# A fourth unit of the sequence DFT as block products, and four weight units prepared in the feed-forward

## The chip, the core and the metric

The kernel runs on one core of one Trainium2 chip. The time is the device time of one execution in microseconds, as the median of several runs; lower is better. The engines are TensorE (PE in the profile, its weight loads PEld), VectorE (DVE), ScalarE (ACT), GpSimd (POOL) and SyncE (SP), which here only issues DMAs, all from one queue in order.

## What is computed

One layer: an FNet mixing step and a gated feed-forward, each behind a layer norm and with a residual. There are 2048 tokens of 448 features, 1792 hidden features, all float32.

```python
def _A_ref(x, dft_seq_re, dft_seq_im, dft_hid_re, dft_hid_im):
    a = jnp.einsum("bsd,ed->bse", x, dft_hid_re)
    b = jnp.einsum("bsd,ed->bse", x, dft_hid_im)
    return jnp.einsum("ts,bse->bte", dft_seq_re, a) - jnp.einsum("ts,bse->bte", dft_seq_im, b)

def _B_ref(x, w_gate, w_up, w_down):
    g = jnp.einsum("bsd,df->bsf", x, w_gate)
    u = jnp.einsum("bsd,df->bsf", x, w_up)
    return jnp.einsum("bsf,fd->bsd", _gelu(g) * u, w_down)

h = x + _A_ref(_layernorm(x, axis=-1), ...)
h2 = h + _B_ref(_layernorm(h, axis=-1), ...)
```

## The kernel before

**Numbers.** Every float32 operand of a matmul is split into a high and a low float16 part: ACT writes the high part (`hi_part`, L100), DVE the low part as the source less the high part (`lo_part`, L104 without and L106 with a scale). A product is three matmuls: high by high, high by low, low by high.

**First step.** The tokens are 16 tiles of 128, taken in pairs; a pair is a unit u of 0 to 7, in the order 0, 1, 5, 2, 6, 3, 7, 4 (`ORDER`). A tile is normed, split, transposed, and multiplied by the hidden DFT (`feature_mm`, L421, result `ab`), and `feature_out` writes its float16 operands `b`.

**Sequence DFT.** It has eight passes p of 256 output tokens; each pass adds up, over the eight units u, a block of DFT weights `w_seq` (raw `wr`, split `ws`) times that unit's `b` (`seq_mm`, L517). A unit has one of two forms:

- plain: 24 matmuls of 448 columns; its weights are four blocks and are split as they are (1024 columns on ACT and on DVE);
- in `S_UNITS` (units 5, 6, 7): seven block products in the manner of Strassen, 42 matmuls of 224 columns. DVE first adds up four of seven weight blocks (`seq_sums`, three instructions, L479 to L481, tile `wsum`); the split covers seven blocks (256, 512 and 1024 columns). In the first step such a unit's tiles go to a float32 tile `b32` in the pool `ring` (tag `w`, two buffers), POOL makes four sums of blocks (`feature_sums`, L459 to L461), and the split covers seven blocks (1568 columns) where a plain tile's covers 2 x 448.

**Order.** All of this is a list of slots: `("F", i)` for tile i of the first step and `("U", p, u)` for a unit of a pass. Units of pass 0 stand between the F slots. `plan(n, rank, what)` puts work ahead of slot n; a unit's sums are planned three slots ahead, its split two slots ahead, its load six. The order so written is the order on every engine.

**Gate and up weights.** They come in 14 units f of 128 hidden features. For each, `Weights(f)` fetches raw weights (two DMAs, tile `gu_raw`), `sums` makes block sums on DVE (tile `gu_s`, L579 to L582), `split` writes both halves (tile `gu_w`, in `ring`, the one that `b32` uses too), and `store` writes the result to `w_dram`. All 14 are planned into the first step and the DFT: one early (unit 13, four slots behind the second seven-product unit), the others spread evenly from three slots behind the first step's end.

**Feed-forward.** It has four quarters q of 512 tokens and 14 units f in each, so tiles t = 0 to 55; tile t has three accumulators X, Y, Z (L927). `gw[t]` holds its weights: the first three are left from the DFT, the others are loaded from `w_dram` (`gw_load`). In the first quarter eight of them pass through a buffer `ahead` of four places, which has the size of a quarter's hidden values `hh`. The down product (L869) starts with the second quarter; in the first, `down_prep` prepares its weights: POOL makes sums (`wd_s`, L210 to L213), ACT and DVE split. In the first quarter the body of tile t is:

```python
cur.x_close()      # X += ...; ACT: gelu of X (g1)
nxt.x_open()       # X of t+1; ACT: copy it into Y of t+1 (L966)
prev.c_last()
cur.y_mid()        # Y += ...; ACT: u3; DVE: hidden values
nxt.z_open()
nxt.y_open()       # Y of t+1 += ...
cur.y_close()
cur.z_close()
down_prep(t - 1)   # at odd t: ACT splits wd and, once POOL is done, wd_s
```

(comments added here). X, Y and Z alternate between two sets of banks from tile to tile.

Of the kernel before, what the change touches and what calls it, by code (L numbers as in the profile page):

```python
# [8 lines left out]
F16 = mybir.dt.float16  # L9
F32 = mybir.dt.float32  # L10
# [3 lines left out]
P = 128  # L14
S, D, DF = 2048, 448, 1792
NT = S // P
NF = DF // P
# [10 lines left out]
W_SC = 256.0  # L28
# [4 lines left out]
def kernel(  # L33
# [37 lines left out]
    nc = tc.nc  # L71
# [9 lines left out]
    ps_dft = right.enter_context(tc.tile_pool(name="ps_dft", bufs=4, space=bass.MemoryType.PSUM))  # L81

    ident = const.tile([P, P], F16, name="ident")
# [15 lines left out]
    def hi_part(dst, src, scale=1.0):  # L99
        A.activation(dst, src, AF.Copy, scale=scale)  # L100
# [67 lines left out]
    def w_tile(name, pool):  # L168
        return pool.tile([P, 28 * P], F16, tag="w", bufs=2 if pool is ring else 1, name=name)
# [119 lines left out]
    dft = right.enter_context(tc.tile_pool(name="dft", bufs=1, side="right"))  # L289

    N_PASS, N_UNIT = 8, 8
    S_UNITS, WR = (5, 6, 7), 3
# [5 lines left out]
    first = ExitStack()  # L298
    p2 = right.enter_context(tc.tile_pool(name="p2", bufs=1, side="right"))
    p1 = first.enter_context(tc.tile_pool(name="p1", bufs=1, side="right"))  # L300
# [262 lines left out]
    def h_store(p):  # L563
        nc.sync.dma_start(h_dram[p], hp[divmod(p, 2)])


    class Weights:


        def __init__(self, f):  # L570
            self.f = f
            self.raw = p2.tile([P, 2, 6, P], F32, tag="raw", name=f"gu_raw{f}")
            for r in range(2):
                nc.sync.dma_start(self.raw[:, r], w_gu[f, :, r])

        def sums(self):
            gate, up = self.raw[:, 0], self.raw[:, 1]
            s = self.s = p2.tile([P, 10, P], F32, tag="s", name=f"gu_s{self.f}")
            V.tensor_add(s[:, 0:3], up[:, 0:3], up[:, 3:6])  # L579
            V.tensor_sub(s[:, 3:6], s[:, 0:3], gate[:, 0:3])  # L580
            V.tensor_sub(s[:, 6:8], gate[:, 0:2], up[:, 0:2])
            V.tensor_sub(s[:, 8:10], gate[:, 4:6], s[:, 4:6])  # L582
# [14 lines left out]

        def split(self, of_raw):
            if of_raw:
                self.w = w_tile(f"gu_w{self.f}", ring if self.f != 2 else ring3)  # L600
# [23 lines left out]
    for n, s in zip((2, 5, 7), S_UNITS):  # L624
        mixed.insert(n, s)
# [4 lines left out]
    gu = {}  # L630
# [5 lines left out]
    def plan(n, rank, *what):  # L636
        at(todo, n, *((rank, w) for w in what))
# [43 lines left out]
    plan(0, 9, lambda: gu.update({order[0]: Weights(order[0])}))  # L681
    for k, f in enumerate(order):
        n = at_f[k]
        plan(n, 7, lambda f=f: gu[f].sums())
        plan(n + 1, 7, lambda f=f: gu[f].split(True))
        if k + 1 < NF:
            plan(n + 2, 9, lambda f=order[k + 1]: gu.update({f: Weights(f)}))
        plan(n + 2, 7, lambda f=f: gu[f].split(False))
        plan(n + 3, 10, lambda f=f: gu[f].store())
# [112 lines left out]
    for n in sorted(todo):  # L802
        for _, what in sorted(todo.pop(n), key=lambda t: t[0]):
            what()
    seq_out(N_PASS - 1)
    h_store(N_PASS - 1)
    down_load(1)
    gw = {f: gu[f].w for f in range(3)}
    right.close()


    right.close()
# [65 lines left out]
    fpool = ctx.enter_context(tc.tile_pool(name="fpool", bufs=1, side="right", reuse_waits="tile"))  # L878
# [129 lines left out]
    ahead = fpool.tile([P, 4, 28 * P], F16, tag="hh", bufs=2, name="gw_ahead")  # L1008

    def gw_load(t):  # L1010
        if 3 <= t < 7 or 10 <= t < 14:
            gw[t] = ahead[:, (t - 3) % 7]
        else:
            gw[t] = w_tile(f"gw{t}", ring if t % 3 else ring3)
        nc.sync.dma_start(gw[t], w_dram[t % NF])

# [52 lines left out]
    def last_begin():  # L1069
        last["h"] = fpool.tile([P, 2, NF, 2 * TQ], F16, tag="hh", bufs=2, name="h_last")  # L1070
# [118 lines left out]
    for t in range(3, 7):  # L1189
        gw_load(t)  # L1190
# [7 lines left out]
    for t in range(N_GU):  # L1198
        q, f = divmod(t, NF)
        if f == 0 and q < 3:  # L1200
            hh[q] = fpool.tile([P, NC, 4, TQ], F32, tag="hh", bufs=2, name=f"hh{q}")
            if 1 <= q <= 2:
                hops_tile(q + 1)
        if 0 < t < 8:
            gw_load(t + 6)
        if NF - 2 <= t < N_GU - 2:
            gw_load(t + 2)
# [12 lines left out]
        if q == 0:  # L1220
# [4 lines left out]
            cur.y_mid()  # L1225
            nxt.z_open()
# [4 lines left out]
            if t > 0:  # L1231
                down_prep(t - 1)
        else:
# [100 lines left out]
```

## Time and profile before

| | |
|---|---|
| runs | 718.6, 719.0, 719.13 us; median 719.0 |
| profiled execution | 718.65 us, span 716.9 us |
| PE busy | 709.5 us, 5800 matmuls |
| PEld, DVE, ACT, POOL busy | 562.2, 500.0, 386.1, 203.2 us |
| DMA | 142.89 MB, mean 199 GB/s |
| granted clock of PE | 1.00 throughout |

The span goes from the first to the last instruction; the profiled execution's own time holds some 1.75 us more around it. A timeline row reads: start, length, engine, line, operation, output tile and inputs, shape, count, and in brackets the idle time of that engine just before, with what ended it. A row with a count covers several instructions.

### The profile page before, as it was taken

Reading aid. Unit: us, or ns where it says so; the run is one execution under the profiler, and the core shown is the slowest. Engines: PE = TensorE matmul, PEld = TensorE weight load, DVE = VectorE, ACT = ScalarE, POOL = GpSimd, SP = SyncE. Lnnn points to the kernel's source line nnn. Section 1 sums busy time; section 2 is a strip of 40 time slices with the busy share of each in tenths; the row PEclk is TensorE's granted clock in tenths of the full one; section 3 lists DMA queues with packets and bytes.
Section 4 is the critical chain, followed back from the end, with each engine's and each line's share of the span. In section 5 each row is a group of like instructions: output and inputs, shape, how many; then the busy total and the mean of one; then the engine's idle time right before and its main releaser. Section 6 shows DMA issues by size and latency. Waiting matters only on the chain.

```text
span 716.9 us, 14587 instructions
## 1 busy us (share of the span) xinstructions
PE 709.5 (99%) x5800; PEld 562.2 (78%) x5800; DVE 500.0 (70%) x1016; ACT 386.1 (54%) x818; POOL 203.2 (28%) x235
## 2 busy tenths in 40 slices
PE   8999999999999999999999999999999999999998
PEld 5556556676767666676788889999999999999998
DVE  6777859898989887888345667575765756677520
ACT  5575644765665654646155565555555545555500
POOL 0023120000000000010015564374664755557230
PEclk9999999999999999999999999999999999999999
DMA  9464444896969699685089525647466576655401
GB/s 329 105 147 94 106 152 143 298 264 250 306 232 307 232 272 351 215 305 172 1 336 354 187 101 161 190 163 203 174 188 194 187 215 209 212 179 206 155 15 65
DMA packets 72339, 142.89 MB, mean 199 GB/s; under 512 B 41296, under 2 KB 47568, under 8 KB 72272
## 3 DMA queue, kind: packets, MB, share of 16 engines
q1 hardware_dynamic: 72272, 141.97, 61.3%
q8 instruction: 45, 0.74, 0.4%
q14 instruction: 22, 0.18, 0.1%
HBM read 112.46 MB, written 20.19 MB: 185 GB/s over the span
## 4 chain that ended last, share of the span: by engine, by line
PE 83%; DVE 8%; ACT 5%; DMA 2%; issue 1%; SPq 0%; ACTq 0%; DVEq 0%
PE acc L517 36%; PE pY L927 14%; PE acc_d L869 11%; PE pZ L927 9%; PE pX L927 9%; ACT b L100 1%; DVE xs L104 1%; PE last_Z L1098 1%; PE last_X L1098 1%; PE last_Y L1098 1%; DVE st_x L327 1%; ACT x L354 1%; ACT xs L100 1%; DMA w_dram<-gu_w 1%; DMA wh_raw<-in_w_hid_dram 1%
## 5 line engine op out<-in xcount | busy, mean ns | idle before, releaser
L517 PE MATMUL acc<-b,ws 128*128 128x448 f16 (+1 forms) x1968 | 279.4, 305 | 0.2 <-DVE ws L106 0.2
L517 PEld LDWEIGHTS <-ws 128*128 128x128 f16 x1968 | 190.4, 98 | 88.7 <-DVE ws L106 0.8
L927 PEld LDWEIGHTS <-gw 128*128 128x128 f16 x1755 | 171.5, 98 | 17.7 <-issue 0.8
L927 PE MATMUL pY<-hops,gw 128*128 128x256 f16 x765 | 105.2, 273 | 0.0
L869 PE MATMUL acc_d<-wd,dn_w 128*128 128x224 f16 x882 | 105.1, 259 | 0.0
L100 ACT ACTIVATE ws<-wr 128x1024 f16<-128x1024 f32 (+2 forms) x88 | 64.3, 756 | 46.9 <-issue 26.2
L869 PEld LDWEIGHTS <-dn_w 128*128 128x128 f16 x882 | 85.1, 98 | 2.8
L106 DVE SCALAR_TENSOR_TENSOR ws<-wr,ws 128x1024 f16<-128x1024 f32 (+2 forms) x88 | 73.8, 861 | 19.1 <-ACT ws L100 18.5
L1006 POOL TENSOR_TENSOR hh<-hh,c 128x256 f32<-128x256 f32 x42 | 31.8, 759 | 141.9 <-ACT c L1004 141.9
L210 POOL TENSOR_TENSOR wd_s<-wd 128x448 f32<-128x448 f32 x7 | 7.9, 1134 | 224.8 <-DMA w_dram<-gu_w 207.8
L927 PE MATMUL pZ<-hops,gw 128*128 128x256 f16 x495 | 68.7, 273 | 0.4 <-DVE hh L937 0.3
L927 PE MATMUL pX<-hops,gw 128*128 128x256 f16 x495 | 68.4, 273 | 0.0
L421 PEld LDWEIGHTS <-xT 128*128 128x128 f16 x352 | 34.2, 98 | 32.7 <-issue 1.5
L104 DVE TENSOR_TENSOR dn_w<-hh,dn_w 128x256 f16<-128x256 f32 x42 | 19.6, 466 | 53.1 <-ACT dn_w L100 53.1
L1029 POOL TENSOR_TENSOR dn_s<-hh 128x256 f32<-128x256 f32 x42 | 52.9, 1258 | 0.0
L971 ACT ACTIVATE u<-pY 128x256 f32<-128x256 f32 x56 | 21.5, 384 | 55.7 <-PE pY L927 55.6
L104 DVE TENSOR_TENSOR dn_w<-dn_s,dn_w 128x640 f16<-128x640 f32 x42 | 46.3, 1102 | 6.2 <-ACT dn_w L100 5.0
L966 ACT ACTIVATE pY<-pX 128x256 f32<-128x256 f32 x56 | 20.7, 369 | 49.2 <-PE pX L927 49.1
L421 PE MATMUL ab<-wh_hi,xT 128*128 128x448 f16 x224 | 45.6, 352 | 0.6 <-ACT xT L384 0.4
L1028 POOL TENSOR_TENSOR dn_s<-hh 128x256 f32<-128x256 f32 x42 | 38.0, 904 | 0.0
L985 ACT ACTIVATE u<-pY 128x256 f32<-128x256 f32 x56 | 21.5, 383 | 26.9 <-PE pY L927 26.6
L860 POOL TENSOR_TENSOR hr<-hr,v 128x224 f32<-128x224 f32 x48 | 33.4, 717 | 0.1
(137 smaller groups left out, 971.2 us busy)
## 6 DMA issues: line engine op xcount, KB each, us to landing
gw<-w_dram SPq DMA_DIRECT2D x45, 896.0 KB, 5.0
wr<-in_w_seq_dram SPq DMA_DIRECT2D x64, 512.0 KB, 4.6
w_dram<-gu_w SPq DMA_DIRECT2D x14, 896.0 KB, 7.5
gu_raw<-in_w_gu_dram SPq DMA_DIRECT2D x28, 384.0 KB, 5.6
gw_ahead<-w_dram SPq DMA_DIRECT2D x8, 896.0 KB, 7.5
wd<-in_w_down_dram SPq DMA_DIRECT2D x14, 448.0 KB, 4.4
hx<-in_x_dram SPq DMA_DIRECT2D x8, 448.0 KB, 6.9
h_dram<-hx SPq DMA_DIRECT2D x8, 448.0 KB, 6.8
```

What stands on the lines that cost most here:

```text
L100: A.activation(dst, src, AF.Copy, scale=scale)
L104: V.tensor_sub(dst, src, hi)
L106: V.scalar_tensor_tensor(dst, src, scale, hi, op0=ALU.mult, op1=ALU.subtract)
L421: PE.matmul(feat[i][r][:, :D], xT[i][:, kx, :], w[:, kw, r * D : (r + 1) * D], start=n == 0, stop=n == 10,)
L517: PE.matmul(banks[k][:, cols], lhs, rhs, start=k not in begun, stop=stop, skip_group_check=True)
L860: op(x, x, m)
L869: PE.matmul(acc[k // 2][:, k % 2 * HD : (k % 2 + 1) * HD], a_of(la, a), b_of(lb, b), start=first and m == 0 and k % 2 == 0, stop=last and ...
L927: PE.matmul(ps, w[:, wl, wa + ws, :], ops[:, m + ms, :], start=first and n == 0, stop=last and n == len(terms) - 1, skip_group_check=True,)
L1006: G.tensor_mul(c22, c22, self.c12)
L1028: G.tensor_add(s[:, 0:2], t[:, 0:2], t[:, 2:4])
L1029: G.tensor_sub(s[:, 2:4], t[:, 1:4:2], t[:, 0:4:2])
L1098: PE.matmul(banks[0][:, c * HD : (c + 1) * HD] if one else banks[c][:, 0:HD], last["h"][:, lh, f, tok], w, start=f == 0 and m == 0 and c = ...
```

## The change

`S_UNITS` becomes (4, 5, 6, 7), so unit 4, the last of the first step, takes the seven-product form. In a pass the units now stand as 0, 1, 4, 2, 5, 3, 6, 7 (before: 0, 1, 5, 2, 3, 6, 4, 7). Its larger operands need room. So the gate/up units 4, 7, 10 and 13 are no longer prepared in the DFT: they are prepared in the first quarter, from tiles t = 0, 3, 6 and 9 on, in six beats each, two per tile (`late_prep`, `Weights.beat`), and are used where they were made as well as stored. The buffer `ahead` goes away; a pool `scr` holds raw weights, sums and two weight tiles in the first quarter, and the second quarter's hidden values take its place (`odd_q`). In the DFT two gate/up units (12 and 11) are early, and the other eight are spread from 15 slots behind the first step's end. The transposing constant `ident` moves to a pool that is closed after the first step.

```diff
-    S_UNITS, WR = (5, 6, 7), 3
+    S_UNITS, WR = (4, 5, 6, 7), 3
...
+        def beat(self, k):
+
+            if k < 2:
+                self.sums(k == 0, k == 1)
+            if k == 1:
+                self.w = self.w_of()
+            parts = self.parts(True) + self.parts(False)
+            if k > 1:
+                s0, s1, src = parts[k - 2]
+                lo_part(self.slots(1, s0, s1, src), src, self.slots(0, s0, s1, src), W_SC)
+            if 0 < k < 5:
+                s0, s1, src = parts[k - 1]
+                hi_part(self.slots(0, s0, s1, src), src, W_SC)
...
-    for n, s in zip((2, 5, 7), S_UNITS):
+    for n, s in zip((2, 4, 6, 7), S_UNITS):
...
-    early_f = [s + 4 for s in pairs[1:2]]
-    n0 = p1_end + 3
-    order = list(reversed(range(2, NF))) + [0, 1]
-    late_f = NF - len(early_f)
+    early_f = [s + 4 for s in pairs[1:3]]
+    n0 = p1_end + 15
+    LATE = {4: 0, 7: 6, 10: 12, 13: 18}
+    in_dft = [f for f in range(NF) if f not in LATE]
+    N_DFT = len(in_dft)
+    order = list(reversed(in_dft[2:])) + in_dft[:2]
...
+    fpool = ctx.enter_context(tc.tile_pool(name="fpool", bufs=1, side="right", reuse_waits="tile"))
+    quarter0 = ExitStack()
+    scr = quarter0.enter_context(tc.tile_pool(name="scr", bufs=1, side="right", reuse_waits="tile"))
+
+    def gw_tile(t):
+        name = f"gw{t}"
+        if t < NF and t % 5 >= 3:
+            return w_tile(name, scr) if t % 5 == 3 else scr.tile([P, 28 * P], F16, tag="stage", name=name)
+        return w_tile(name, ring3 if (t % 5 == 2 if t < NF else t % 3 == 1) else ring)
...
+    gw_load(3)
     seq_out(N_PASS - 1)
+    gu_late(min(LATE))
     h_store(N_PASS - 1)
     down_load(1)
...
-    for t in range(3, 7):
-        gw_load(t)
+    late_beats = {n + k: (f, k) for f, n in LATE.items() for k in range(6)}
...
+        f, k = late_beats[beat]
+        gu[f].beat(k)
+        after = [v for v in LATE if v > f]
+        if k == 3 and after:
+            gu_late(after[0])
+        if k == 5:
+            gu[f].store()
+            gw[f] = gu[f].w
...
-            hh[q] = fpool.tile([P, NC, 4, TQ], F32, tag="hh", bufs=2, name=f"hh{q}")
+            if q == 1:
+                quarter0.close()
+                odd_q = ctx.enter_context(tc.tile_pool(name="odd_q", bufs=1, side="right"))
+            hh[q] = (fpool, odd_q)[q % 2].tile([P, NC, 4, TQ], F32, tag="hh", name=f"hh{q}")
...
-        if 0 < t < 8:
-            gw_load(t + 6)
-        if NF - 2 <= t < N_GU - 2:
-            gw_load(t + 2)
+        ahead = {1: 5, 2: 6, 4: 8, 5: 9, 7: 11, 8: 12, 10: 14, 12: 15, 13: 16}.get(t) if t <= NF else t + 2
+        if ahead and ahead < N_GU:
+            gw_load(ahead)
...
             cur.y_mid()
+            late_prep(2 * t)
             nxt.z_open()
             nxt.y_open()
             cur.y_close()
@@
             if t > 0:
                 down_prep(t - 1)
+            late_prep(2 * t + 1)
```

DVE's order at the end of the first step, before, from pass 1's unit 0 on. In the names, `ws0_7` is the split weight of pass 0, unit 7, `b8` and `b9` are the operands of unit 4's tiles 8 and 9, and the numbers behind are running ones.

```order
L106 SCALAR_TENSOR_TENSOR ws1_0_1183<-wr1_0_770,ws1_0_1183 128x1024
L479 TENSOR_TENSOR wsum0_7_1186<-wr0_7_912 128x512
L480 TENSOR_TENSOR wsum0_7_1186<-wsum0_7_1186,wr0_7_912 128x256
L481 TENSOR_TENSOR wsum0_7_1186<-wsum0_7_1186,wr0_7_912 128x256
L106 SCALAR_TENSOR_TENSOR b9_1216<-ab9_0_1192,b9_1216 128x448
L106 SCALAR_TENSOR_TENSOR b9_1216<-ab9_1_1193,b9_1216 128x448
L106 SCALAR_TENSOR_TENSOR ws0_7_1221<-wr0_7_912,ws0_7_1221 128x256
L106 SCALAR_TENSOR_TENSOR ws0_7_1221<-wr0_7_912,ws0_7_1221 128x512
L106 SCALAR_TENSOR_TENSOR ws0_7_1221<-wsum0_7_1186,ws0_7_1221 128x1024
L106 SCALAR_TENSOR_TENSOR ws0_4_1258<-wr0_4_1033,ws0_4_1258 128x1024
```

The same place in the changed kernel, from the last piece of unit 7's split on (ahead of that split the four sums of gate/up unit 11, L581 to L587, now stand):

```order
L111 SCALAR_TENSOR_TENSOR ws0_7_1225<-wsum0_7_1187,ws0_7_1225 128x1024
L109 TENSOR_TENSOR b8_1232<-b32_8_1178,b8_1232 128x1568
L480 TENSOR_TENSOR wsum0_4_1238<-wr0_4_1033 128x512
L481 TENSOR_TENSOR wsum0_4_1238<-wsum0_4_1238,wr0_4_1033 128x256
L482 TENSOR_TENSOR wsum0_4_1238<-wsum0_4_1238,wr0_4_1033 128x256
L111 SCALAR_TENSOR_TENSOR gu_w11_1242<-gu_raw11_1035,gu_w11_1242 128x512
L111 SCALAR_TENSOR_TENSOR gu_w11_1242<-gu_raw11_1035,gu_w11_1242 128x256
L111 SCALAR_TENSOR_TENSOR ws0_4_1277<-wr0_4_1033,ws0_4_1277 128x256
L111 SCALAR_TENSOR_TENSOR ws0_4_1277<-wr0_4_1033,ws0_4_1277 128x512
L111 SCALAR_TENSOR_TENSOR ws0_4_1277<-wsum0_4_1238,ws0_4_1277 128x1024
L109 TENSOR_TENSOR b9_1284<-b32_9_1222,b9_1284 128x1568
```

Between unit 7's sums and the last piece that unit 4's matmuls of pass 0 need, the sums and first split of gate/up unit 11 now stand, and unit 4's own work has grown from five instructions to eight.

ACT's order behind tile 7 of the first quarter, before. `wd` are down weights, `g1_8` is the gelu of tile 8's X, `pY_9` the copy of tile 9's X into its Y, `c12` and `u3` are the hidden values' parts.

```order
L100 ACTIVATE wd_4083<-wd32_3_4410 128x448
L100 ACTIVATE wd_4083<-wd_s_3_4534 128x1120
L980 ACTIVATE g1_8_4602<-pX_8_4546 128x256
L966 ACTIVATE pY_9_4611<-pX_9_4604 128x256
L1004 ACTIVATE c12_7_4592<-c12_7_4592 128x256
```

The same in the changed kernel:

```order
L105 ACTIVATE wd_4235<-wd32_3_4583 128x448
L105 ACTIVATE wd_4235<-wd_s_3_4719 128x1120
L105 ACTIVATE gw10_4725<-gu_s10_4685 128x512
L1023 ACTIVATE g1_8_4801<-pX_8_4736 128x256
L1009 ACTIVATE pY_9_4810<-pX_9_4803 128x256
L1047 ACTIVATE c12_7_4784<-c12_7_4784 128x256
```

One split of unit 10's weights now stands between the down weights and the gelu. Behind tiles 3 and 9 it is the same with units 7 and 13; behind tiles 5 and 11 none stands there.

More of the change, by code (lines that the diff above doesn't have):

```diff
@@ L80 @@
     right = ctx.enter_context(ExitStack())
-    ps_dft = right.enter_context(tc.tile_pool(name="ps_dft", bufs=4, space=bass.MemoryType.PSUM))
-    ident = const.tile([P, P], F16, name="ident")
+    banks_dft = ExitStack()
+    ps_dft = banks_dft.enter_context(tc.tile_pool(name="ps_dft", bufs=4, space=bass.MemoryType.PSUM))
+    dft = right.enter_context(tc.tile_pool(name="dft", bufs=1, side="right"))
+    p2 = right.enter_context(tc.tile_pool(name="p2", bufs=1, side="right"))
+    first = ExitStack()
+    p1 = first.enter_context(tc.tile_pool(name="p1", bufs=1, side="right"))
+    ident = p1.tile([P, P], F16, name="ident")
     make_identity(nc, ident)
```

59 lines of the change are left out of this document (32 added, 27 removed).

## The prediction

> **What bounds the kernel now.** I read the page first, the busy table and then the chain that ended last; after that the chain in order of time.
>
> ```profile
> PE 709.5 (99%) x5800; PEld 562.2 (78%) x5800; DVE 500.0 (70%) x1016; ACT 386.1 (54%) x818; POOL 203.2 (28%) x235
> ...
> 101.33 256.32 PE acc L517 x1810
> ```
>
> TensorE is busy 709.5 of 716.9 us, and from 101.33 the chain stays on the sequence DFT for 256.32 us without a break. Then two stretches by windows (length, then busy time of PE, PEld, DVE, ACT, POOL, then clock, DMA share and GB/s):
>
> ```profile
> 360.00:418.00 58.00, 57.98 (x531) 51.72 (x529) 31.39 (x56) 35.07 (x85) 26.33 (x31) 1.00 0.73 278
> 187.60:222.40 34.80, 34.80 (x248) 23.84 (x247) 31.13 (x64) 21.98 (x42) 0.00 (x0) 1.00 0.85 267
> ```
>
> The first is nearly all of the feed-forward's first quarter: PE misses 0.02 us. The second is one pass of the DFT: DVE is at 31.13 of 34.80, and PE misses nothing. So a matmul saved is a gain, and a wait made anywhere is a loss of its own length; PE has no idle time that could take it up.
>
> **The gain, on PE.** What a matmul takes in a stream is read from starts, since ends are modelled. From the timeline of PE:
>
> ```profile
> 28.49 4.70 PE L517 MATMUL acc<-b,ws 128*128 128x448 f16 x24
> 33.03 2.81 PE L421 MATMUL ab<-wh_hi,xT 128*128 128x448 f16 x14
> ...
> 63.06 4.19 PE L517 MATMUL acc<-b,ws 128*128 128x224 f16 x42
> 67.09 2.81 PE L421 MATMUL ab<-wh_hi,xT 128*128 128x448 f16 x14
> ```
>
> A plain unit's 24 matmuls of 448 columns take 33.03 - 28.49 = 4.54 us (189 ns each); a seven-product unit's 42 of 224 columns take 67.09 - 63.06 = 4.03 us (96 ns each). Unit 4 changes form in all 8 passes: 8 x 0.51 = 4.08 us less. Both forms already run on this line, so I give this term 0.1 us either way.
>
> The Trainium skill ("TensorE: Matmul & The Clock Gate", Back-to-back issue gap) speaks against this: it gives a stream of load-and-matmul pairs 81 ns at 128 columns and 131 ns at 512. On a straight line between these, as an estimate, 224 columns take 93.5 ns and 448 take 123, a seven-product unit 3.93 us against 2.94, and the eight of them would cost 7.9 us. The trace agrees at 224 columns (96 ns) and not at 448 (189 ns); the measurement decides.
>
> **End of the first step: a new wait.** Unit 4 is transformed last there. Its two tiles now need sums on POOL and a split of 1568 columns, its share of pass 0 needs sums, and a second gate/up unit (11) is prepared in the same place. What stands there before, on ACT and then on DVE:
>
> ```profile
> 95.10 0.98 ACT L100 ACTIVATE b<-ab 128x448 f32<-128x448 f32 x2 [7.57 <-DMA w_dram<-gu_w]
> ```
>
> ```profile
> 79.53 0.55 DVE L579 TENSOR_TENSOR gu_s<-gu_raw 128x384 f32<-128x384 f32 x1
> ...
> 81.26 1.15 DVE L106 SCALAR_TENSOR_TENSOR b<-ab,b 128x448 f16<-128x448 f32 x2
> ...
> 84.45 1.02 DVE L106 SCALAR_TENSOR_TENSOR gu_w<-gu_raw,gu_w 128x512 f16<-128x512 f32 x2
> 85.39 1.02 DVE L106 SCALAR_TENSOR_TENSOR ws<-wr,ws 128x256 f16<-128x256 f32 x2
> ...
> 87.46 1.29 DVE L106 SCALAR_TENSOR_TENSOR gu_w<-gu_s,gu_w 128x512 f16<-128x512 f32 x2
> 97.51 2.17 DVE L104 TENSOR_TENSOR b<-b,b 128x1568 f16<-128x1568 f32 x1 [8.76 <-ACT b L100]
> 99.60 1.68 DVE L106 SCALAR_TENSOR_TENSOR ws<-wr,ws 128x1024 f16<-128x1024 f32 x1
> 101.77 1.79 DVE L104 TENSOR_TENSOR b<-b,b 128x1568 f16<-128x1568 f32 x1 [0.50 <-ACT b L100]
> 103.48 1.15 DVE L106 SCALAR_TENSOR_TENSOR b<-ab,b 128x448 f16<-128x448 f32 x2
> ...
> 105.67 0.69 DVE L479 TENSOR_TENSOR wsum<-wr 128x512 f32<-128x512 f32 x1
> ...
> 107.20 1.15 DVE L106 SCALAR_TENSOR_TENSOR b<-ab,b 128x448 f16<-128x448 f32 x2
> 108.26 1.02 DVE L106 SCALAR_TENSOR_TENSOR ws<-wr,ws 128x256 f16<-128x256 f32 x2
> 109.20 1.22 DVE L106 SCALAR_TENSOR_TENSOR ws<-wsum,ws 128x1024 f16<-128x1024 f32 x1
> 110.33 2.35 DVE L106 SCALAR_TENSOR_TENSOR ws<-wr,ws 128x1024 f16<-128x1024 f32 x2
> ```
>
> ACT stands 7.57 us for the store of the gate/up unit whose ring buffer tile 15 needs. DVE idles 8.76 us behind it, and from 97.51 it only just keeps ahead of PE:
>
> ```profile
> 100.62 0.54 PE L517 MATMUL acc<-b,ws 128*128 128x448 f16 x2
> 101.33 8.87 PE L517 MATMUL acc<-b,ws 128*128 128x448 f16 x46 [0.16 <-DVE ws L106]
> ```
>
> Two matmuls of 0.19 us from 100.62 would end at 101.00; the third starts at 101.33, so 0.33 us was waited. The new order is the old one up to tile 15's split. From its end, 103.48, I lay rows end to end, each at its length from start to start: a 1568-column split 103.48 - 101.77 = 1.71; the sums of a seven-product unit 107.20 - 105.67 = 1.53; its split 110.33 - 108.26 = 2.07, of it 0.94 for the two short pieces; a 1024-column split 110.33 - 109.20 = 1.13; gate/up sums 81.26 - 79.53 = 1.73; their first split 85.39 - 84.45 = 0.94. DVE then finishes: pass 1's unit 0 at 104.7, sums of unit 7 at 106.25, gate/up sums at 108.0, split of unit 7 at 110.05, tile 8 at 111.75, sums of unit 4 at 113.3, gate/up split at 114.2, unit 4's short pieces at 115.2, its long one at 116.3, tile 9 at 118.0. ACT's halves and POOL's sums come earlier than each of these.
>
> PE reaches unit 4 at 100.62 + 0.33 + 4.54 + 4.54 + 4.03 = 114.1. Its third matmul needs the short pieces: 1.0 us waited. The ninth needs the long piece (due 115.8, there 116.4): 0.55. The twenty-third needs tile 9 (due 117.7, there 118.1): 0.4. That is 1.9 us. What follows in DVE's queue (the rest of unit 11, pass 1's unit 1) is there in time to a tenth.
>
> POOL now sums tiles 8 and 9 beside this. For tile 15 it looked so:
>
> ```profile
> 96.15 1.13 POOL L459 TENSOR_TENSOR b<-b 128x448 f32<-128x448 f32 x1 [4.93 <-ACT b L100]
> 97.36 0.66 POOL L460 TENSOR_TENSOR b<-b 128x224 f32<-128x224 f32 x1
> 98.11 2.09 POOL L461 TENSOR_TENSOR b<-b 128x224 f32<-128x224 f32 x1
> ```
>
> Meanwhile DVE's split took 99.60 - 97.51 = 2.09 in place of 1.71 and the next one 1.68 in place of 1.22: 0.84 us lost. Two tiles can so cost 0 to 1.7; I take 0.5, nearer to nothing, as DVE's sums use other forms than that split. The term is 2.4 us. Bounds: -0.3 (even today's 0.33 goes) and 6.8 (1.9, and DVE stopped for all of POOL's 2 x 2.45 us, with 0.66 for the last piece).
>
> **The passes.** Per pass DVE takes on 1.53 + 2.07 - 1.13 = 2.47 us for unit 4, 17.3 over passes 1 to 7; it loses five of the thirteen gate/up units there, at 1.73 + 0.94 + 1.2 (the 1.29 row less 0.1 of overlap) = 3.9 each: 19.4. Beside a pass shorter by 0.5 us its share stays about that of the window above, under which PE never waited. I take 0. Two seven-product units now stand side by side, 3.6 us of DVE each against 4.03 of PE: up to 1 us if gate/up work falls on them.
>
> **The first quarter.** Four units are prepared there in six beats each. For DVE that is 3.9 us in three tiles of 4.26 us (396.21 - 379.18 below, over four), beside 31.39 of 58: covered. ACT is not idle where it counts. At odd tiles it waits for POOL's sums of the down weights, and only behind these stand the gelu, the copy of X into Y, and PE's product on Y:
>
> ```profile
> 378.66 0.38 ACT L966 ACTIVATE pY<-pX 128x256 f32<-128x256 f32 x1
> ...
> 394.38 1.14 ACT L100 ACTIVATE wd<-wd_s 128x1120 f16<-128x1120 f32 x1 [0.72 <-POOL wd_s L213]
> 395.42 0.37 ACT L980 ACTIVATE g<-pX 128x256 f32<-128x256 f32 x1
> 395.69 0.38 ACT L966 ACTIVATE pY<-pX 128x256 f32<-128x256 f32 x1
> ```
>
> ```profile
> 379.18 1.36 PE L927 MATMUL pY<-hops,gw_ahead 128*128 128x256 f16 x11
> ...
> 396.21 1.36 PE L927 MATMUL pY<-hops,gw 128*128 128x256 f16 x11
> ```
>
> ```profile
> L100 ACT ACTIVATE gu_w<-gu_raw 128x512 f16<-128x512 f32 x14 | 8.6, 615 | 0.0
> ```
>
> The copy ends at 396.07, 0.14 us before PE uses it, and 0.14 at 379.18 too. The new order puts a 512-column split (0.615, less 0.1 of overlap) between that wait and the gelu behind tiles 3, 7 and 9, so the copy comes 0.51 later and PE waits about 0.45 (0.08 of hand-over counted): 3 x 0.45 = 1.35. Behind tile 1 POOL's sums are long done, behind 5 and 11 no split stands.
>
> The raw weights of unit 10 are fetched when unit 7's second piece is split at tile 4 and are wanted at tile 6:
>
> ```profile
> 381.58 1.33 DVE L106 SCALAR_TENSOR_TENSOR wd<-wd_s,wd 128x1120 f16<-128x1120 f32 x1
> ...
> 388.23 0.42 DVE L937 SCALAR_TENSOR_TENSOR hh<-pZ,u 128x256 f32<-128x256 f32 x1 [1.82 <-ACT u L985]
> ```
>
> ```profile
> gu_raw<-in_w_gu_dram SPq DMA_DIRECT2D x28, 384.0 KB, 5.6
> w_dram<-gu_w SPq DMA_DIRECT2D x14, 896.0 KB, 7.5
> ```
>
> With tile 4's wait of 0.45 the fetch starts at 382.91 + 0.45 + 0.33 = 383.7 and lands 5.6 us later, at 389.3; DVE wants it at 388.65 + 0.45 = 389.1. DVE waits 0.2 in front of the gate/up sums, and by way of the down-weight split, POOL and ACT some 0.3 reaches PE at tile 8. So 1.65. Bounds: 0 (a gain is excluded by the 0.02) and 4.2 (that fetch 2.5 us later, as a store's 7.5 and a place behind one allow).
>
> SP's queue: unit 3's load and the first raw pair now stand ahead of the last store of h; both wait only for buffers that DVE frees two units before the DFT ends, so nothing behind them is late. Later the load of tile 14's weights waits for tile 10's matmuls, with a down-weight load (wanted three tiles on) and unit 13's store behind it; that store frees the place of the second quarter's hidden values, 7.5 us after tile 11, which is before tile 14 writes them. Weight loads come two to five tiles ahead, and seven loads, four raw pairs and four stores move about what eleven loads and one more fetch moved at a DMA share of 0.73. All this: 0, and the whole delay if one comes late.
>
> **Sum.** -4.08 + 2.4 + 0 + 1.65 = 0.0 on the profiled execution's 718.65 us (span 716.9). The median of the runs, 719.0, is 0.35 above it. I forecast 718.9.
>
> **Rivals.** *Hidden after all*, faster. DVE rows overlap more closely than I laid them, or the ring store lands sooner and DVE starts with a lead. For it: at 31.13 of 34.80 DVE did not stop PE once. Against it: 97.51 starts with no lead, and the wait of 0.33 stands there already. One of the two sets of waits gone leaves 719.0 - 4.08 + 1.65 = 716.6, or with 2.4 717.3; both gone, 714.9. *POOL stops DVE*, slower: beside tiles 8 and 9 DVE stands for all of POOL's 4.9 us in place of 0.5, and the time is 719.0 + 4.4 = 723.4; it decides from 2 us lost on. For it: the 2.09 us rows on both engines. Against it: tile 15's three instructions cost 0.84. *No gain on PE*: at 108 ns a narrow matmul would give nothing back, 719.0 + 4.05 = 723; the row at 96 ns, 42 in a stream, leaves it 0.01.
>
> The Trainium skill ("SBUF — State Buffer", SBUF: two separate sides) calls the port pair that VectorE and GpSimd share an exclusive lock, which the loser waits for through the whole instruction. By that rule the time is the 723.4 of the second rival; the trace agrees in part, with 0.84 of tile 15's 2.45 us. By the first page's rule the third would stand at 719.0 + 7.9 + 4.05 = 731, which 189 ns excludes.
>
> **Chances.** The forecast 0.56; its own range is 717.6 to 720.4, 0.2% or 1.4 us, about what a measurement can tell from no change. Hidden 0.27. Slower 0.17: POOL 0.08, late fetches or bursts in the passes 0.08 (1 and 2.5 us make 722.5 at worst), no gain 0.01. The range reaches down to one set of waits gone, 716.3, and up to half of POOL's price, 721.4.
>
> **What would show it.** PE should have 192 fewer wide and 336 more narrow matmuls, still 189 and 96 ns apart. The DFT should show waits for DVE of about 2.4 us in all between 113 and 121, none later, and end near 356.0 where it ended at 101.33 + 256.32 = 357.65. In the first quarter PE should wait three times, ahead of the products on Y of tiles 5, 9 and 11, by 0.4 to 0.8 us. No wait at 114 makes the second term wrong, a quarter without waits the third; a wait of 5 us at 114 makes POOL right.

## The result, and the profile after

The changed kernel takes 729.15 us (median of 4 runs, 728.99 to 729.76), the kernel before on the same chip 718.9: a ratio of 1.0144, 95% interval 1.0127 to 1.0162. It is 10.3 us slower; the forecast was 718.9, range 716.3 to 721.4. The profiled execution took 729.15 us too, its span 727.4. From its page:

```profile
PE 708.2 (97%) x5944; PEld 574.1 (79%) x5944; DVE 529.1 (73%) x1054; ACT 396.1 (54%) x836; POOL 215.3 (30%) x241
```

PE has 144 matmuls more (336 narrow ones for 192 wide ones) and is busy 1.3 us less in a span 10.5 us longer: it waits. Three starts on PE cut the span: the first matmul behind the first step, the first of the feed-forward (pX), and the first of the down product (acc_d), which begins the second quarter. In the changed kernel, with the waits of the DFT between them (start, length, ..., in brackets the idle time and what ended it):

```profile
100.84 9.70 PE L518 MATMUL acc<-b,ws 128*128 128x448 f16 x50
111.85 1.06 PE L518 MATMUL acc<-b,ws 128*128 128x224 f16 x6 [1.31 <-DVE ws L111]
113.58 3.62 PE L518 MATMUL acc<-b,ws 128*128 128x224 f16 x36 [0.67 <-DVE ws L111]
118.08 1.06 PE L518 MATMUL acc<-b,ws 128*128 128x224 f16 x6 [0.88 <-DVE ws L111]
119.82 1.51 PE L518 MATMUL acc<-b,ws 128*128 128x224 f16 x14 [0.67 <-DVE ws L111]
121.52 24.32 PE L518 MATMUL acc<-b,ws 128*128 128x224 f16 x181 [0.18 <-DVE b L109]
146.16 0.59 PE L518 MATMUL acc<-b,ws 128*128 128x224 f16 x3 [0.33 <-DVE ws L111]
147.64 4.39 PE L518 MATMUL acc<-b,ws 128*128 128x224 f16 x42 [0.89 <-DVE ws L111]
152.71 7.59 PE L518 MATMUL acc<-b,ws 128*128 128x224 f16 x56 [0.67 <-DVE ws L111]
...
361.58 0.82 PE L970 MATMUL pX<-hops,gu_w 128*128 128x256 f16 x6
...
430.30 0.93 PE L913 MATMUL acc_d<-wd,dn_w 128*128 128x224 f16 x8
```

The same two starts in the kernel before (its first, 100.62, is in the prediction):

```profile
357.49 0.82 PE L927 MATMUL pX<-hops,gu_w 128*128 128x256 f16 x6
...
419.90 0.93 PE L869 MATMUL acc_d<-wd,dn_w 128*128 128x224 f16 x8
```

So the DFT stretch takes 361.58 - 100.84 = 260.74 us (before 256.87), the first quarter 430.30 - 361.58 = 68.72 (before 62.41), and the rest 297.1 (before 297.0). 3.87 us are lost in the DFT, where 4.08 should have been won, and 6.31 in the first quarter. Without any wait the DFT stretch would take 256.87 - 4.08 - 0.33 (the wait of before) = 252.46, so 8.28 us of it are waits. By the rows, five stand at the end of the first step (111.85 to 121.52, 3.71 us by the brackets): two at unit 7, ahead of its third and ninth matmul, and three at unit 4, ahead of its third, ninth and twenty-third. Three more stand at the end of pass 1 (146.16 to 152.71, 1.89). A bracket leaves out the end of the last matmul, which the profile draws some 0.3 us too long (three narrow ones of 0.096 take 0.59 at 146.16). Counted from start to start, at 189 and 96 ns for a matmul, the two groups are about 5.4 and 2.9 us.

### The profile page after: what moved, and what is told of

It reads as the page before. It is cut to its first block, busy times and chain, and to the rows that moved or that the text cites. A ratio compares the mean times of both kernels' runs of the same rounds, so it can differ in the third digit from the quotient of the medians.

```text
span 727.4 us, 14930 instructions
## 1 busy us (share of the span) xinstructions
PE 708.2 (97%) x5944; PEld 574.1 (79%) x5944; DVE 529.1 (73%) x1054; ACT 396.1 (54%) x836; POOL 215.3 (30%) x241
## 4 chain that ended last, share of the span: by engine, by line
PE 73%; DVE 13%; ACT 8%; issue 3%; DMA 2%; POOL 1%; SPq 0%; ACTq 0%; DVEq 0%
PE acc L518 29%; PE pY L970 13%; PE acc_d L913 11%; PE pX L970 8%; PE pZ L970 8%; DVE ws L111 2%; ACT ws L105 2%; ACT b L105 1%; DVE xs L109 1%; DVE st_x L328 1%; PE last_Z L1132 1%; PE last_X L1132 1%; PE last_Y L1132 1%; DVE b L109 1%; ACT x L355 1%
## 5 line engine op out<-in xcount | busy, mean ns | idle before, releaser
L518 PE MATMUL acc<-b,ws 128*128 128x224 f16 (+1 forms) x2112 | 277.4, 293 | 6.0 <-DVE ws L111 5.4
L518 PEld LDWEIGHTS <-ws 128*128 128x128 f16 x2112 | 202.8, 98 | 80.2 <-DVE ws L111 9.5
L970 PEld LDWEIGHTS <-gw 128*128 128x128 f16 x2067 | 201.9, 98 | 27.8 <-issue 7.3
L970 PE MATMUL pY<-hops,gw 128*128 128x256 f16 x901 | 122.5, 273 | 5.1 <-ACT pY L1009 5.1
L111 DVE SCALAR_TENSOR_TENSOR ws<-wr,ws 128x256 f16<-128x256 f32 (+2 forms) x96 | 73.4, 790 | 19.3 <-ACT ws L105 18.7
L105 ACT ACTIVATE ws<-wr 128x256 f16<-128x256 f32 (+2 forms) x96 | 63.0, 690 | 39.9 <-PE acc L518 21.5
L970 PE MATMUL pZ<-hops,gw 128*128 128x256 f16 x583 | 81.0, 273 | 0.8 <-DVE hh L980 0.7
L105 ACT ACTIVATE ws<-wsum 128x1024 f16<-128x1024 f32 x32 | 33.6, 1050 | 35.1 <-DVE wsum L482 35.0
L1014 ACT ACTIVATE u<-pY 128x256 f32<-128x256 f32 x56 | 21.5, 383 | 52.2 <-PE pY L970 52.1
L111 DVE SCALAR_TENSOR_TENSOR ws<-wsum,ws 128x1024 f16<-128x1024 f32 x32 | 39.1, 1222 | 2.6 <-ACT ws L105 2.6
```

Of the source, the lines that this page charges most:

```text
L111: V.scalar_tensor_tensor(dst, src, scale, hi, op0=ALU.mult, op1=ALU.subtract)
L518: PE.matmul(banks[k][:, cols], lhs, rhs, start=k not in begun, stop=stop, skip_group_check=True)
L970: PE.matmul(ps, w[:, wl, wa + ws, :], ops[:, m + ms, :], start=first and n == 0, stop=last and n == len(terms) - 1, skip_group_check=True,)
L1014: A.activation(self.u2, self.Y, AF.Copy, scale=SC)
```

## The experiments

All times are medians, beside the kernel before on the same chip. The table gives the two stretches for each kernel, from the same three starts, in its one profiled execution.

| kernel | us | before | DFT stretch | quarter |
|---|---|---|---|---|
| before | | | 256.87 | 62.41 |
| changed | 729.15 | 718.9 | 260.74 | 68.72 |
| late units alone (e1) | 724.49 | 718.79 | 257.00 | 67.99 |
| no late preparation (e2) | 723.12 | 718.79 | 261.06 | 62.41 |
| late: ScalarE's part (e3) | 724.18 | 718.79 | 260.98 | 63.65 |
| late: VectorE's part (e4) | 727.22 | 718.79 | 261.45 | 66.48 |
| no sums of tiles 8, 9 (e5) | 726.08 | 718.6 | 257.53 | 68.72 |
| one early unit (e6) | 726.84 | 718.6 | 258.66 | 67.98 |
| split of sums later (e7) | 725.41 | 718.6 | 260.86 | 64.06 |
| and no early unit (e8) | 725.81 | 718.6 | 261.39 | 63.95 |
| and ten units spread (e9) | 722.72 | 718.56 | 257.92 | 64.01 |
| e9, units in turn (e10) | 729.48 | 718.56 | 265.52 | 63.96 |
| e9, beats reordered (e11) | 724.67 | 718.56 | 257.92 | 66.76 |
| e10 and e11 (e12) | 732.75 | 718.56 | 265.52 | 67.11 |
| changed, sums a slot earlier (e13) | 728.07 | 718.73 | 260.02 | 67.97 |
| e9, norm's bias first (e14) | 721.04 | 718.73 | 256.57 | 64.67 |
| e9, sums a slot earlier (e15) | 718.6 | 718.73 | 253.78 | 65.25 |
| e14 and e15 (e16) | 717.37 | 718.73 | 252.41 | 65.05 |
| e16, raw halves first (e17) | 717.65 | 718.57 | 252.41 | 64.79 |

### Do the two parts add up?

The first kernel has unit 4 plain, with the order and the early unit of before:

```diff
-    S_UNITS, WR = (4, 5, 6, 7), 3
+    S_UNITS, WR = (5, 6, 7), 3
```

> S_UNITS, the order of units and the early gate/up unit as before; only the four gate/up units are prepared in the first quarter. The two parts are taken to be independent, the first quarter's price being 6.1 to 6.4 us: 718.9 + 6.2 = 725.1 us, the DFT ending at 357.4 to 357.7, waits ahead of the products on Y of tiles 5, 7, 9, 11 and 13. If instead the first quarter's waits came from work that the slower DFT left over: 719 to 720.

The second leaves the late beats out and loads in their place:

```diff
     def late_prep(beat):
...
+        return
         f, k = late_beats[beat]
...
-        ahead = {1: 5, 2: 6, 4: 8, 5: 9, 7: 11, 8: 12, 10: 14, 12: 15, 13: 16}
+        ahead = {1: 5, 2: 6, 3: 7, 4: 8, 5: 9, 6: 10, 7: 11, 8: 12, 9: 13, 10: 14, 12: 15, 13: 16}
```

> The changed kernel without the late preparation: units 4, 7, 10 and 13 are not computed, and the quarters load a neighbouring unit's stored weights in their place. Independent parts: the DFT ends at 361.7 as in the changed kernel, the first quarter waits 0.3 us or less, 729.15 - 6.2 = 723.0 us. If the parts depend on each other: 725 to 729.

Measured 724.49 and 723.12: the price of each part is its own, 5.6 us for the quarter (67.99 - 62.41) and 4.2 for the DFT (261.06 - 256.87). With no late work the quarter is back at 62.41 to the hundredth, so the other buffers, the order of loads and the larger operands cost it nothing. Together the parts cost 0.4 us more than one by one. In the quarter it is 0.73 (68.72 - 67.99), all of it at one place: tile 7's product on Y waits 1.00 us by its bracket in the changed kernel and 0.26 with the late units alone.

### The first quarter: whose work?

```diff
-        gu[f].beat(k)
+        if 0 < k < 5:
+            hi_part(gu[f].hi[...], r[:, a : a + (s1 - s0) * P], W_SC)
```

> The kernel without late preparation, plus ScalarE's four splits of each late unit alone (same sizes and beats, read from the raw weights, result not used); VectorE does no late work. Theory 'queue order' (the splits stand ahead of gelu and copy on ScalarE): most of the 6.2 us come back, 727 to 729. Theory 'port' (VectorE and GpSimd slow each other in SBUF): three waits of 0.45 us, 724.0 to 724.7, and GpSimd's sums of the down weights stay at 1.13, 1.13 and 0.66 us.

```diff
-        gu[f].beat(k)
+        if k < 2:
+            gu[f].sums(k == 0, k == 1)
+        if k > 1:
+            lo_part(d, part, h, W_SC)
```

> The kernel without late preparation, plus VectorE's part of each late unit alone (four sums, four low parts, same sizes and beats, result not used); ScalarE does no late work. Theory 'port': GpSimd's sums lengthen to 1.3 to 1.5 us, 726 to 728.5. Theory 'queue order': 723.0 to 723.5, since VectorE has idle time at every tile.

ScalarE's part adds 1.24 us to the quarter, VectorE's 4.07, both as 'port' has it. The rows of the down-weight sums, which GpSimd makes and neither kernel changes (min/median/max ns), first with ScalarE's part, then with VectorE's:

```profile
L215 POOL TENSOR_TENSOR wd_s<-wd x7: 1128/1135/1137, 309.7 to 423.6; 128x448 f32<-128x448 f32 x7
L217 POOL TENSOR_TENSOR wd_s<-wd x7: 1128/1135/1322, 310.8 to 424.7; 128x448 f32<-128x448 f32 x7
L218 POOL TENSOR_TENSOR wd_s<-wd x7: 652/662/1105, 312.1 to 425.8; 128x224 f32<-128x224 f32 x7
```

```profile
L215 POOL TENSOR_TENSOR wd_s<-wd x7: 1128/1193/1463, 310.2 to 426.9; 128x448 f32<-128x448 f32 x7
L217 POOL TENSOR_TENSOR wd_s<-wd x7: 1134/1447/1583, 311.3 to 428.0; 128x448 f32<-128x448 f32 x7
L218 POOL TENSOR_TENSOR wd_s<-wd x7: 652/972/1112, 312.5 to 429.1; 128x224 f32<-128x224 f32 x7
```

By the medians three sums take 2.93 us in the one and 3.61 in the other. In the changed kernel, VectorE's rows and then GpSimd's at one place show why:

```profile
378.34 0.69 DVE L111 SCALAR_TENSOR_TENSOR gw<-gu_s,gw 128x512 f16<-128x512 f32 x1
379.38 1.06 DVE L581 TENSOR_TENSOR gu_s<-gu_raw 128x384 f32<-128x384 f32 x1
380.47 1.38 DVE L582 TENSOR_TENSOR gu_s<-gu_s,gu_raw 128x384 f32<-128x384 f32 x1
381.77 0.41 DVE L1039 SCALAR_TENSOR_TENSOR hh<-pY,g 128x256 f32<-128x256 f32 x1
...
378.56 1.47 POOL L215 TENSOR_TENSOR wd_s<-wd 128x448 f32<-128x448 f32 x1 [3.13 <-issue]
379.98 1.45 POOL L217 TENSOR_TENSOR wd_s<-wd 128x448 f32<-128x448 f32 x1
381.39 0.97 POOL L218 TENSOR_TENSOR wd_s<-wd 128x224 f32<-128x224 f32 x1
```

The two take turns, one whole instruction each. GpSimd's second sum ends at 381.43; VectorE's second, which takes 0.56 alone, ends at 381.85, 0.42 after it, and GpSimd's third, which takes 0.66 alone, ends 0.51 after that. What each waits for the other lies inside its row as busy time. ScalarE's split then comes late, and behind it gelu, copy, and PE's product on Y, five times; the rows of waits for it (total us, times, longest):

```profile
PE pY L970 <- ACT pY L1009: 5.1, 5, 1.2
...
ACT wd L105 <- POOL wd_s L218: 9.0, 5, 2.0
```

If so, the sums need only more time until somebody waits for them:

```diff
+                down_hi(n, 1)
                 down_lo(n, 1)
...
             down_lo(n, 0)
-            if n < NC - 1:
-                down_hi(n, 1)
```

> The changed kernel with ScalarE's split of the down-weight sums issued one tile later, so that GpSimd's sums have a tile more before anyone waits. VectorE and GpSimd work as before. Theory 'port by way of the late sums': the first quarter's waits go but for ScalarE's own splits, 723.5 to 724.7. If the waits come from lengthened work on VectorE or ScalarE itself: 727 to 729.

The quarter falls to 64.06: 4.66 of the 6.31 us come back, with the same work. GpSimd's sums are as long as before (1.51, 1.45 and 0.98 us from 378.24 on), but nobody waits for them. The median, 725.41, lies 0.7 over the end of what was expected, in runs from 724.48 to 726.46; the stretch is the cleaner measure. What stays is 1.65. It is not ScalarE's part: no product on Y waits any more, since ScalarE's late splits do not stand behind a wait for GpSimd either. PE's waits in this quarter are all for VectorE:

```profile
384.86 0.71 PE L969 MATMUL pZ<-hops,gw 128*128 128x256 f16 x5 [0.49 <-DVE hh L979]
...
397.99 0.70 PE L969 MATMUL pZ<-hops,gw 128*128 128x256 f16 x5 [0.20 <-DVE hh L979]
...
409.51 0.81 PE L969 MATMUL pZ<-hops,gw 128*128 128x256 f16 x6 [0.44 <-DVE c L979]
```

### The end of the first step

VectorE, then GpSimd's sums of tiles 8 and 9, in the changed kernel:

```profile
103.72 2.06 DVE L111 SCALAR_TENSOR_TENSOR ws<-wr,ws 128x1024 f16<-128x1024 f32 x1
105.70 1.14 DVE L480 TENSOR_TENSOR wsum<-wr 128x512 f32<-128x512 f32 x1
106.87 0.77 DVE L481 TENSOR_TENSOR wsum<-wsum,wr 128x256 f32<-128x256 f32 x1
107.67 1.24 DVE L482 TENSOR_TENSOR wsum<-wsum,wr 128x256 f32<-128x256 f32 x1
108.84 1.01 DVE L581 TENSOR_TENSOR gu_s<-gu_raw 128x384 f32<-128x384 f32 x1
109.88 0.90 DVE L582 TENSOR_TENSOR gu_s<-gu_s,gu_raw 128x384 f32<-128x384 f32 x1
...
102.81 1.88 POOL L460 TENSOR_TENSOR b<-b 128x448 f32<-128x448 f32 x1 [2.49 <-ACT b L105]
...
109.51 0.86 POOL L462 TENSOR_TENSOR b<-b 128x224 f32<-128x224 f32 x1
```

```diff
         b = b32[i]
+        if i // 2 == 4:
+            A.activation(b[:, 4:8], b[:, 0:4], AF.Copy)
+            return
```

> The changed kernel with GpSimd's sums of tiles 8 and 9 left out (ScalarE copies other halves into their place, so the sums are not computed); VectorE's work is the same. Theory 'port': VectorE's rows from 103.7 on return to 1.22, 0.69, 0.42, 0.43, 0.55 and 0.56 us (3.25 us less in sum), the DFT ends 2.5 to 3.5 us earlier, 725.7 to 726.7. Theory 'backlog' (VectorE simply has too much to do there, contention 0.5 us): 728.5 to 729.2.

726.08, as 'port' has it. The same VectorE rows without GpSimd beside them:

```profile
103.93 1.23 DVE L111 SCALAR_TENSOR_TENSOR ws<-wr,ws 128x1024 f16<-128x1024 f32 x1
105.07 0.68 DVE L483 TENSOR_TENSOR wsum<-wr 128x512 f32<-128x512 f32 x1
105.79 0.42 DVE L484 TENSOR_TENSOR wsum<-wsum,wr 128x256 f32<-128x256 f32 x1
106.25 0.42 DVE L485 TENSOR_TENSOR wsum<-wsum,wr 128x256 f32<-128x256 f32 x1
106.59 0.55 DVE L584 TENSOR_TENSOR gu_s<-gu_raw 128x384 f32<-128x384 f32 x1
107.17 0.56 DVE L585 TENSOR_TENSOR gu_s<-gu_s,gu_raw 128x384 f32<-128x384 f32 x1
```

7.12 us of rows become 3.86: 3.26 us lost to GpSimd, and the DFT stretch is shorter by 260.74 - 257.53 = 3.21. The two waits at unit 7 are gone. What is left there are the three at unit 4, ahead of its third, ninth and twenty-third matmul, 2.1 us from start to start; the waits at the end of pass 1 stay as they were.

```diff
-    early_f = [s + 4 for s in pairs[1:3]]
+    early_f = [s + 4 for s in pairs[1:2]]
```

> The changed kernel with one early gate/up unit (12) in place of two; unit 11 goes among the eight in the passes. Both theories: VectorE has 3.9 us less to do at the first step's end and the waits there (about 5.2 us) go. If the waits at the end of pass 1 (about 2.9 us) are the rest of the same backlog, they go too: 721 to 722. If they are made in pass 1 by itself: 724 to 725.

726.84: neither case. One unit (3.9 us of VectorE) fewer leaves waits at 112.83, 118.40 and 120.36 and, by about 1.7 us, at the end of pass 1, and a new one of 0.67 at 219.79; the DFT stretch gains 2.08. Waits here do not go down one for one with VectorE's work. Ahead of this stretch the profile is 0.9 us late (its first start is 101.71 in place of 100.84), which counts in its time and not in the stretch.

### The passes: room, or queues in order?

From here on the kernels have the later split of the sums too, but for the one that is said to be made on the changed kernel itself. First no early unit:

```diff
-    early_f = [s + 4 for s in pairs[1:3]]
+    early_f = [s + 4 for s in pairs[1:1]]
```

> The edit of the run before, and no early gate/up unit at all: ten in the passes, so no store stands before tile 15's buffer (VectorE was idle 8.8 us there). If VectorE's lead at the first step's end is what lacks: DFT ends at 353.5 to 354.5, 715 to 717, faster than the kernel before. If ten units are too much for the passes: 718 to 722.

725.81, slower than both cases. Now nothing waits before 193.95, at the end of the first step or in passes 1 and 2, but the waits come back in passes 3 and 4. With units 3.9 slots apart (the texts on record reckon 3.7, and 4.9 for what are 5.1 below) the raw weights arrive late (VectorE, then PE):

```profile
189.23 0.56 DVE L581 TENSOR_TENSOR gu_s<-gu_raw 128x384 f32<-128x384 f32 x1 [5.32 <-DMA gu_raw<-in_w_gu_dram]
...
193.95 1.34 PE L518 MATMUL acc<-b,ws 128*128 128x224 f16 x6 [1.84 <-DVE ws L111]
```

```diff
-    n0 = p1_end + 15
+    n0 = p1_end + 3
```

> The run with no early gate/up unit, its ten units now spread from 3 slots behind the first step's end (4.9 slots apart) instead of from 15 (3.7 apart). In the 15-slot run VectorE stood 5.3 us for one unit's raw weights. Theory 'raw weights late in a queue in order': the waits of the passes mostly go, 716 to 718.5. Theory 'VectorE has no room in passes 1 to 4': they stay near 5 us or move, 722 to 726.

722.72, in the range of 'no room'; the runs further on show that it is something else. No wait for raw weights is left in the DFT and the stretch gains 3.47, but it still loses 5.5, now in passes 1 and 2.

```diff
+        turn = mixed if p == 1 else (0, 4, 1, 5, 2, 6, 3, 7)
```

> The run above with plain and seven-product units in turn (0, 4, 1, 5, 2, 6, 3, 7) from pass 2 on, so that units 6 and 7 no longer stand side by side. Theory 'side by side': what waits are left at the ends of passes go, 0.5 to 2 us below the run above. Theory 'total work of VectorE in the pass': within 0.4 us of it.

729.48: against both theories the DFT loses 7.6 us more, at twelve waits. That units 6 and 7 stand side by side is not the cause; why this order is so much worse was not tested further.

A place at the end of pass 1 in the changed kernel shows another cause (ScalarE's rows, then VectorE's):

```profile
133.95 1.06 ACT L105 ACTIVATE ws<-wsum 128x1024 f16<-128x1024 f32 x1 [4.73 <-DVE wsum L482]
...
138.56 1.04 ACT L105 ACTIVATE ws<-wr 128x1024 f16<-128x1024 f32 x1
143.14 1.41 ACT L228 ACTIVATE xn_h<-hx,nb_h,r_h 128x448 f32<-128x448 f32 x2 [3.55 <-DVE nb_h L147]
...
139.63 1.23 DVE L111 SCALAR_TENSOR_TENSOR ws<-wr,ws 128x1024 f16<-128x1024 f32 x1 [3.37 <-ACT ws L105]
...
142.61 0.43 DVE L482 TENSOR_TENSOR wsum<-wsum,wr 128x256 f32<-128x256 f32 x1
142.95 0.15 DVE L147 SCALAR_TENSOR_TENSOR nb_h<-mv_h,r_h 128x2 f32<-128x2 f32 x1
...
144.89 1.21 DVE L111 SCALAR_TENSOR_TENSOR ws<-wr,ws 128x256 f16<-128x256 f32 x2 [1.78 <-ACT ws L105]
```

ScalarE stands 4.73 us at the split of weight sums that VectorE has not made yet; the moments of h and the next split stand behind it, and VectorE waits 3.37 for that split. Then ScalarE waits 3.55 for a bias of 0.15 us that stands on VectorE behind the next unit's weight sums, and VectorE waits 1.78 for what stands behind that. Neither is full. So the next two edits take no work away, only the waits for each other. The first is made on the changed kernel itself, and then on the run with ten units spread; the second on that run alone, and then both together:

```diff
-            plan(n - 3, 6, lambda p=p, u=u: seq_sums(p, u))
+            plan(n - 4, 6, lambda p=p, u=u: seq_sums(p, u))
```

> The changed kernel with the weight sums of each seven-product unit planned four slots ahead instead of three, so that ScalarE's split no longer comes to the sums before VectorE has made them. Work is the same. Theory 'queues in order' (pass 1's end waits because ScalarE and VectorE wait for each other in turn, though neither is busy all the time): the 2.9 us there mostly go, 726 to 727.5. Theory 'VectorE has no room': 728.7 to 729.5.

728.07. The waits at the end of pass 1 are gone: behind 127.08 PE runs through. ScalarE's waits for weight sums, in the changed kernel and in this one:

```profile
ACT ws L105 <- DVE wsum L482: 35.0, 17, 4.7
```

```profile
ACT ws L105 <- DVE wsum L482: 1.8, 2, 1.3
```

But the time is over the range, since the edit also moves sums at the end of the first step, ahead of a plain unit's split that PE needs, and beside GpSimd: that split, 1.23 us long without GpSimd's sums, takes 2.15 from 107.21 on, and PE waits 2.36 for it.

```diff
         plan(n + 2, 5, lambda q=q, j=j: ffn_rstd(q, j))
+        if q < 2:
+            plan(n + 2, 5, lambda q=q, j=j: ffn_bias(q, j))
```

> The run with ten units spread (722.7 us), with the small instruction that ScalarE's norm of h waits for put ahead of a seven-product unit's weight sums on VectorE instead of behind them (1.5 us earlier). Theory 'queues in order': the wait for it falls from 3.55 to about 2 us and pass 1 gives back 1 to 2 us: 720.7 to 721.7. Else 722.5 to 723.

> The run with ten units spread, with the weight sums planned four slots ahead. Theory 'queues in order': the five waits of passes 1 and 2 (5.5 us in all) mostly go, 717.5 to 720. Theory 'VectorE has no room': 722 to 723.5.

> Both edits of the two runs before together. Theory 'queues in order': 716.5 to 719, at or below the kernel before (718.7); the first quarter still holds about 1.6 us of waits. Theory 'VectorE has no room': 721 to 723.

721.04, 718.6 and 717.37: all three as 'queues in order' has it. With both edits the chain of waits shows the whole DFT as one piece, where the changed kernel's began at 152.71:

```profile
101.25 252.41 PE acc L527 x1956
```

The DFT stretch is 353.50 - 101.09 = 252.41, against 252.46 worked out for no wait at all. In the window from 122 to 152, busy times of PE, PEld, DVE, ACT in the changed kernel and in this one:

```profile
122.00:152.00 30.00, 28.77 (x223) 20.75 (x220) 23.67 (x49) 15.70 (x32) 0.00 (x0) 1.00 0.60 201
```

```profile
122.00:152.00 30.00, 30.00 (x243) 23.33 (x242) 28.94 (x61) 21.14 (x41) 0.00 (x0) 1.00 0.71 225
```

PE waited while VectorE was busy 23.67 of 30 us, and does not wait at 28.94. This kernel is faster than the one before: 0.9977, interval 0.9966 to 0.9988. Its quarter still takes 2.64 us too much, where about 1.6 was expected.

### What is left in the quarter

In the next, made on the run with ten units spread, VectorE's part of the mid-tile beat stands behind `z_close`, and the raw halves are split first:

```diff
-            late_prep(2 * t)
+            late_prep(2 * t, lo=False)
...
             cur.z_close()
+            late_prep(2 * t, hi=False)
```

> The run before the last with the late units' beats in another order: raw halves first, so the next raw weights are fetched half a tile earlier, and VectorE's part of the beat in mid-tile stands behind the hidden values instead of ahead of them. Theory 'what is left in the first quarter (about 1.6 us) is VectorE's late work ahead of hidden values': the quarter takes 62.4 to 63.0 us instead of 63.95, 1 to 1.5 us less. If ScalarE's splits make it: within 0.4 us.

> All edits together: no early unit, ten spread, units in turn, split of the sums a tile later, the new beats. If every wait found is gone: 718.7 - 4.4 + 0.3 = 714.6; with some left, 715 to 717. If VectorE's total is the bound in the passes: 718 or more.

724.67 fits neither case, and 732.75 only the open end of the last. In the first the quarter takes 2.75 us more, and PE then waits up to 1.3 us for hidden values, which now stand behind two beats at the tile's end. The second has units in turn as well, and loses what that lost.

In the last, made on the run with both queue edits, the first large sum is in beat 0, the second in 1, the small ones in 2, and every split a beat earlier:

```diff
+            if k == 0:
...
+                V.tensor_add(s[:, 0:3], up[:, 0:3], up[:, 3:6])
+            if k == 1:
+                V.tensor_sub(self.s[:, 3:6], self.s[:, 0:3], gate[:, 0:3])
+            if k == 2:
+                self.sums(False, True)
```

> The run with both queue edits (717.4 us), whose DFT has no wait left; its first quarter takes 65.05 us where the kernel before takes 62.41. The late beats stay where they are, but the raw halves are split first (so the next raw weights are fetched half a tile earlier) and the two large sums of a unit go to two beats. Theory 'raw weights late, and sums ahead of hidden values' (VectorE stood 1.95 and 0.53 us for raw weights): the quarter takes 62.7 to 64.0 us, 715.4 to 716.5. Theory 'any late work in mid-tile delays the hidden values': 717 to 718.

717.65 (0.9985, interval 0.9976 to 0.9994). VectorE waits for no raw weights any more, yet the quarter gives back only 0.26 us: three waits of 0.35 to 0.71 by the brackets, for the values that VectorE makes from Z, stay. This fits the second case; that no late work at all can stand in mid-tile without a price is not shown, but a place for it that costs nothing was not found.

## Why the prediction was wrong

**The gain on PE was right.** -4.08 us: the stretch of 252.41 without waits bears it out to 0.05, and the rival "no gain on PE" is out.

**End of the first step: mis-sized.** The term was 2.4 us, of it 1.9 from laying VectorE's rows end to end and 0.5 for GpSimd. The rows were good: with GpSimd's sums away 2.1 is left, at the very three matmuls of unit 4 that the text names. GpSimd's price was wrong: 3.2 us in place of 0.5. The step that failed is "nearer to nothing, as DVE's sums use other forms than that split": VectorE's sums lengthened as its splits did, one of 256 columns from 0.42 to 1.24 us. Nor was tile 15's 0.84 us the price of a whole tile: VectorE stood idle there until 97.51, so only two of its instructions met GpSimd's sums, at some 0.42 each. Beside tiles 8 and 9 it works without a pause, and six met six, at 0.54 each. Unit 7's split, which the text had ready just as PE came to it, so became late as well, which makes two of the five waits. The rival "POOL stops DVE" had the mechanism and a chance of 0.08. It put 4.4 us on top of the forecast; 2.7 came, over the 2 from which it decides. It should have had far more, and the same contention should have been looked for in the quarter, where the change also puts VectorE beside GpSimd.

**The passes: wrong.** 0 was set, since VectorE's busy share stays the same. About 2.9 us were lost at the end of pass 1, and up to 13 in other orders of the same work. The share said nothing of the order: a seven-product unit needs VectorE, ScalarE and VectorE again, in queues that run in order. "None later" is refuted by the rows at 146.16 to 152.71.

**The first quarter: one of two parts.** 1.65 was set and 6.31 measured. The forecast's part, ScalarE's splits ahead of gelu, 1.35, is right: 1.24 measured by itself, in three waits at tiles 5, 9 and 11. The 0.3 for late raw weights did not come: VectorE waits for none in this quarter. The failed step is "3.9 us in three tiles: covered", which counted VectorE's idle time and not that GpSimd's sums are held up beside it: 4.07 us by itself, in five waits behind those sums and one of 0.36 for hidden values. The two together cost about 1.0 more than their sum. Some 0.7 of that is tile 7's wait: GpSimd's third sum there took 1.04 us behind a split of VectorE that had started 0.26 ahead of it, and 0.65 with the late units alone, where it started 0.10 ahead of that split. The rest stays unexplained. The forecast's waits at tiles 5, 9 and 11 became five, one every second tile, as the lengthened sums come every second tile.

**Sum.** -4.08 + 8.28 - 0.33 + 6.31 = 10.2; with 0.2 ahead of the first start and 0.1 behind the last, the span grew by 10.5. The range ended at 721.4, though the text had bounds of 6.8 for the first step and 4.2 for the quarter: they were never added up. Together they give 719.0 - 4.08 + 6.8 + 4.2 = 725.9, still under the measured time. The one term went to 5.4 and the other past its bound, from one cause that the chances held only once, and the passes added 2.9 from another.

## What to carry to other kernels

Before work is put on VectorE under cover of idle time, look whether GpSimd works in the same stretch: lay its rows beside those of VectorE, count the instructions that meet, and charge each meeting (six cost 3.26 us here, of some 4.9 us of GpSimd's own work); then give the result that hangs on GpSimd more time, which here brought back 4.66 of 6.31 us with one line moved. Where two engines hand work to each other in queues that run in order, busy shares do not show whether there is room: read the waits in pairs, and move the producer's piece a slot earlier before taking work away. A change that saves time on the bound engine pays only when these waits are gone: the change that cost 1.4% made the kernel 0.23% faster once the order of the same work was mended.

## What the runs showed of the hardware

VectorE and GpSimd held each other up by whole instructions, both ways: a VectorE sum of 128x384 went from 0.55 to 1.06 us, a GpSimd sum of 128x448 from 1.13 to 1.47. VectorE instructions that take one input from PSUM did not lengthen: the hidden values at 381.77 took 0.41 us beside a GpSimd sum that ran from 381.39 to 382.36, and all 28 of the changed kernel's first quarter took 0.41 to 0.43. This is what the Trainium skill ("SBUF — State Buffer", SBUF: two separate sides) states: an exclusive lock for the whole instruction, which a VectorE instruction takes part in when it runs in a two-port mode, or when both its inputs come from SBUF and the GpSimd instruction reads SBUF. The trace agrees on the two inputs, at 0.42 us from the end of one side's instruction to the end of the other's 0.56 us one; no run here shows the two-port mode. The prediction took tile 15, where only two instructions met GpSimd's sums, for evidence against it.
